# Where the transposition of a unit's exponentials stands: at the head of a slot, or at the end of the slot ahead

## The chip, the cores and the metric

The kernel runs on one core of a Trainium2 chip. The metric is the device time of one execution in microseconds. It computes an attention layer with a sliding window and a few sink keys, and a feed forward layer on its result.

## What is computed

The reference, cut to its core (4 batches, 8 heads, 768 positions, head size 64, `n_sink` 4, `window` 128; 512 columns into 2048 and back):

```python
keep = is_sink | in_window                  # the first 4 keys, and the 128 keys up to the query's own
scores = np.where(keep, scores, -1e9)       # scores = q k^T / 8
a = np.exp(scores - scores.max(-1))
a = a / (a.sum(-1) + 1e-9)
x = (a @ v)                                 # heads side by side: 3072 rows of 512
h = x @ w_in
r = np.maximum(h, 0.0)
out = (s * (r * r) + b) @ w_out
```

## The kernel before

The 3072 rows are worked in 8 chunks of 384 (a batch and a half of its positions). Every float32 operand is split into a high and a low part, and a product is three matmuls (or fewer, with both parts packed into one operand).

**Two streams woven by hand.** `moe_steps` gives 32 steps for a chunk: `l1(f)` makes `h` of 128 of the 2048 columns (12 matmuls, L589), and `l2(f)` adds them into three accumulators `po` (9 matmuls, L608). From the third `l1` on, `l1` and `l2` take turns. Between them stand the slots of the attention of the next chunk; the loop at L768 to L774 issues slot `i` after the first step `j` for which `i * 30 < (j + 1) * (number of slots)`. Chunks 0 and 1 have another, plain attention (`plain_slots`); chunks 2 to 7 have `attn_slots`, which the change touches.

**A slot.** Head `h` has three units (128 queries each), a chunk 24 units, a pair of heads six. Slot `t` works on several units at once:

- `turn` (L324): the transposition, on TensorE, of the exponentials of unit `t - LB` into the last 128 columns of a bank of PSUM, `bank[:, 3 * P:]`.
- `unit_a`: the scores of unit `t` (L303, L304) into the first columns of that same bank, the mask and the maximum on VectorE (L308), the exponential on ScalarE (L314), and two small operations on GpSimd (L317, L318).
- `unit_b`: out of the transposition of unit `t - LB`, the high and low parts `hl` (L337 on VectorE, L339 on ScalarE, L340 on GpSimd; where a unit has no block to its left, L342 and L343 in their place).
- `unit_c`: `o`, the product with the values, of unit `t - LC` (L376, L368). The bank `o` is taken at a head's second unit and read at its third (L384, L385). At a pair's last unit `ts` (L391) is added, and read by L393 and L394.
- `unit_d`: at a pair's last unit, `os` (L402) and `zb` (L404), read by L405 and L406; then `x` of the pair is complete (L407, L408).

With `LB, LC, LD = 3, 6, 2` there are 32 slots. `unit_d` does something in slots 13, 19, 25 and 31.

**The banks.** `ps(...)` takes a tile from `psA`, a pool of five banks of PSUM, for `sc` (the common bank of a slot), `h`, `o`, `ts`, `os` and `zb`. A tile's first write waits until the last reader of the bank's former tile is through. For `sc` the readers are L308 and L337, for `h` L592 and L594. The accumulators `po` have three banks of their own.

**The order.** The framework places semaphores, and a planner of its own orders each engine's instructions: those written earlier go first, but one that the planner's estimate of time sees blocked lets later ones pass. On the chip each engine then works in that order.

Of the kernel before, what the change touches and what calls it, by code (L numbers as in the profile page):

```python
# [15 lines left out]
P = 128  # L16
# [17 lines left out]
RB, VB = 2, 2  # L34
E0 = 8
FN, FB, FC = (4, 2), (6, 6), (9, 10)
LB, LC, LD, L2 = 3, 6, 2, 2


@with_exitstack  # L40
def tile_kernel(ctx, tc, qT, kT, k0, v, vsk, n_sink, window, w, s, b, out):
# [6 lines left out]
    def ps(name):  # L48
        return psA.tile([P, 512], F32, tag="a", name=name)
# [182 lines left out]
    def new_chunk(c):  # L232
        k = Chunk()
        k.c, (k.b, k.half) = c, ORDER[c]
        k.x = [wk.tile([P, NCC, CH], F32R, tag=f"x{i}", name=f"x{i}_{c}") for i in range(2)]
        k.cc, k.xx, k.heads, k.pairs = {}, {}, {}, {}
        return k
# [54 lines left out]
    def unit_a(k, h, i, sc):  # L292

        hd = k.heads[h]
        pp = k.pairs[h // 2]
        g = k.half * BLK + i
        u = (k.c * H + h) * BLK + i
        if k.half == 0:
            c0, n = ((0, 144), (16, 272), (144, 272))[i]
        else:  # L300
            c0, n = ((0, 272), (128, 272), (272, 272))[i]
        qs = slice(i * P, (i + 1) * P)
        nc.tensor.matmul(sc[:, :n], hd.qs[:, qs], hd.kh[:, c0:c0 + n], start=True, stop=False)  # L303
        nc.tensor.matmul(sc[:, :n], hd.qs[:, qs], hd.kl[:, c0:c0 + n], start=False, stop=True)  # L304
        m = m_0 if g == 0 else m_1 if g == 1 else m_odd if g % 2 else m_even
        uu = slice(u, u + 1)
        sm = wk.tile([P, W], F32, name="sm", tag="sm", bufs=SMB)
        nc.vector.tensor_tensor_reduce(out=sm[:, :n], in0=sc[:, :n], in1=m, scale=-0.125, scalar=BIG,  # L308
                                       op0=ALU.add, op1=ALU.min, accum_out=negm[:, uu])

        k.cc[(h, i)] = (sm,) + ((NS, None, 0) if g == 0 else (P, 0, 2 * P) if g % 2 else (P + NS, 0, P))
        s0 = k.cc[(h, i)][3]
        hh = h % 2
        nc.scalar.activation(sm[:, :n], sm[:, :n], AF.Exp, bias=negm[:, uu], scale=-1.0, accum_out=pp.zz[:, i, hh:hh + 1])  # L314
        if g > 0:
            c1, p1 = k.cc[(h, i)][1:3]
            nc.gpsimd.tensor_tensor(out=sm[:, c1:c1 + P], in0=sm[:, p1:p1 + P], in1=sm[:, c1:c1 + P], op=ALU.add)  # L317
        nc.gpsimd.tensor_copy(out=pp.psk[:, i, :6 * NS].rearrange("p (t x) -> p t x", t=3)[:, :, hh * NS:(hh + 1) * NS],  # L318
                              in_=sm[:, s0:s0 + NS].unsqueeze(1).to_broadcast([P, 3, NS]))

    def turn(k, h, i, tp):

        sm, c0 = k.cc[(h, i)][:2]
        nc.tensor.transpose(tp, sm[:, c0:c0 + P], ident)  # L324

    def unit_b(k, h, i, tp):

        sm, c0, p0, _ = k.cc.pop((h, i))
        hd = k.heads[h]
        if i == 0:  # L330
            hd.hl = wk.tile([P, 2, 2 * CH], F32R, name="hl", tag="hl", bufs=HLB)

        a, z = (P if p0 is None else 0), 2 * P
        hi, lo = (hd.hl[:, t, i * z + a:(i + 1) * z] for t in range(2))
        if p0 is not None:
            both = wk.tile([P, 2 * P], F32, tag="two", name="two", bufs=2)
            nc.vector.tensor_tensor(out=both.rearrange("p (s c) -> p s c", s=2), in0=tp.unsqueeze(1).to_broadcast([P, 2, P]), in1=split,  # L337
                                    op=ALU.mult)
            nc.scalar.copy(hi, both)  # L339
            nc.gpsimd.tensor_tensor(out=lo, in0=both, in1=hi.bitcast(F32), op=ALU.subtract)  # L340
        else:
            nc.scalar.copy(hi, tp)  # L342
            nc.vector.tensor_tensor(out=lo, in0=tp, in1=hi.bitcast(F32), op=ALU.subtract)  # L343
        pp = k.pairs[h // 2]
        if h % 2 == 1 and i == BLK - 1:
            zr = wk.tile([P, 2, BLK, 2], F32, tag="zr", name="zr")
            zh = wk.tile([P, BLK, 2], F32R, tag="zh", name="zh")
            nc.vector.tensor_scalar(out=zr[:, 0], in0=pp.zz, scalar1=1e-9, scalar2=None, op0=ALU.add)
            nc.vector.reciprocal(out=zr[:, 1], in_=zr[:, 0])
            nc.vector.tensor_copy(zh, zr[:, 1])  # L350
            nc.gpsimd.tensor_copy(out=pp.psk[:, :, 96:98], in_=zh.bitcast(F32))
            nc.vector.tensor_tensor(out=pp.psk[:, :, 98:100], in0=zr[:, 1], in1=zh.bitcast(F32), op=ALU.subtract)

    def unit_c(k, h, i):

        hd = k.heads[h]
        pp = k.pairs[h // 2]
        cur = i if k.half == 0 else i + 1
        if i == 1:
            hd.o = ps("o")  # L360
            hd.n = 0

        mm = []
        if i == BLK - 1:
            c0 = (2 * i + 1) * P
            nc.tensor.matmul(hd.o[:, i * P:], hd.vv[:, cur, :], hd.hl[:, :, c0:c0 + P], start=False, stop=False)  # L368
        if i > 0:
            mm.append((cur - 1, 2 * i - 1, 2))  # L370
        if i == 1 and k.half == 1:
            mm.append((0, 0, 1))
        for kb, c0, n in mm:
            for t in range(2):
                q0 = c0 // 2 * P
                nc.tensor.matmul(hd.o[:, q0:q0 + n * P], hd.vv[:, kb, :], hd.hl[:, t, c0 * P:(c0 + n) * P],  # L376
                                 start=(hd.n == 0), stop=(i == BLK - 1 and kb == cur - 1 and t == 1))
                hd.n += 1
        if i == BLK - 1:
            a, c = (0, D) if h % 2 == 0 else (D, 0)  # L380
            if h % 2 == 0:
                pp.x = wk.tile([P, CH + P], F32, tag="xm", name="xm", bufs=1)
                pp.y = wk.tile([P, CH + P], F32, tag="y", name="y", bufs=1)
            nc.scalar.copy(pp.y[a:a + D], hd.o[c:c + D])  # L384
            nc.vector.tensor_tensor(out=pp.x[a:a + D], in0=hd.o[a:a + D], in1=pp.y[a:a + D], op=ALU.add)  # L385
            if h % 2 == 1:
                nc.gpsimd.tensor_tensor(out=pp.x[:, CH - P:CH], in0=pp.x[:, CH - P:CH], in1=pp.x[:, CH:], op=ALU.add)
                pp.x = pp.x[:, :CH]
                ts = ps("ts")
                for j in range(BLK):  # L390
                    nc.tensor.transpose(ts[:, j * P:(j + 1) * P], pp.psk[:, j, :], ident)  # L391
                pp.xs = wk.tile([P, CH], F32R, tag="xsk", name="xsk", bufs=1)
                nc.scalar.copy(pp.xs, ts[:, :CH])  # L393
                nc.vector.tensor_tensor(out=pp.xs[32:64], in0=ts[32:64, :CH], in1=pp.xs[32:64].bitcast(F32), op=ALU.subtract)  # L394
# [15 lines left out]
    def attn_slots(c):  # L410
        k = new_chunk(c)
        units, ahead = [], {}
        for pr in range(H // 2):
            h, t0 = 2 * pr, 2 * BLK * pr
            units += [(h + hh, i) for hh in range(2) for i in range(BLK)]
            todo = ((-5, load_pair, pr), (-5, load_keys, h), (-2, load_sinks, pr), (-2, prep_head, h), (-2, load_keys, h + 1),
                    (1, prep_head, h + 1))
            for d, fn, a in todo:
                ahead.setdefault(max(t0 + d, 0), []).append((fn, a))
        n = len(units)  # L420

        def slot(t):
            def f():

                for fn, a in ahead.get(t, ()):
                    fn(k, a)
                bank = ps("sc") if t < n + LB else None
                if 0 <= t - LB < n:
                    turn(k, *units[t - LB], bank[:, 3 * P:])
                if t < n:  # L430
                    unit_a(k, *units[t], bank)
                if 0 <= t - LB < n:
                    unit_b(k, *units[t - LB], bank[:, 3 * P:])
                if 0 <= t - LC < n:
                    unit_c(k, *units[t - LC])
                if 0 <= t - LC - LD < n:
                    unit_d(k, *units[t - LC - LD])
            return f

        return k, [slot(t) for t in range(n + LC + LD)]  # L440


# [300 lines left out]
    k, slots = plain_slots(0)  # L743
# [18 lines left out]
    for c in range(NC_):  # L762
        steps = moe_steps(k.x, store_at(c), wk, before if c == 0 else None, c == NC_ - 1)
        slots = []
        if c + 1 < NC_:
            k, slots = plain_slots(1) if c == 0 else attn_slots(c + 1)
# [58 lines left out]
```

## Time and profile before

| | us |
|---|---|
| median of 3 runs | 745.1 (744.76 to 747.49) |
| the profiled execution, its own time | 745.48 |
| its span, first to last instruction | 743.7 |
| TensorE busy in the span | 707.4 |
| VectorE busy | 507.5 |
| ScalarE busy | 478.7 |
| GpSimd busy | 398.2 |

Times in rows are microseconds from the span's start. PE is TensorE, PEld its weight loads, DVE VectorE, ACT ScalarE, POOL GpSimd. L324 is line 324 of the kernel. An arrow with a name in square brackets says how long the engine stood idle before the row and what released it. The ends of matmuls are modelled and they overlap, so what a matmul costs is read from the distance between starts or ends of neighbours, and a short wait of TensorE may show only there.

### The profile page before, as it was taken

The numbers are of one execution on the slowest core, as the hardware profiler recorded it, in microseconds if no ns is written. First come the engines' busy times: TensorE is split into PE (matmuls) and PEld (weight loads), VectorE is DVE, ScalarE is ACT, GpSimd is POOL, SyncE is SP. The second block draws the span as 40 slices with busy tenths as digits, with TensorE's granted clock in tenths as the row PEclk, the third lists the DMA queues.
The fourth block names the chain that finished last, engine by engine and source line by source line (L and its number), as shares of the span: only waits on it lengthen the run. The fifth ranks groups of instructions, "written<-read, shape, count | busy, mean of one in ns | idle before, by whom it ended". The sixth has DMA issues, their size and how long they took to land.

```text
span 743.7 us, 11974 instructions
## 1 busy us (share of the span) xinstructions
PE 707.4 (95%) x3848; PEld 617.5 (83%) x3848; DVE 507.5 (68%) x1213; ACT 478.7 (64%) x1169; POOL 398.2 (54%) x641
## 2 busy tenths in 40 slices
PE   6788799999999999999999999999999999999996
PEld 3367577789888998899888998899889999889885
DVE  6779999647874778657776678838776568743231
ACT  4978877567774777656774677738675578643222
POOL 2254654358982789626772589816664379710000
PEclk8889989999999999999999999999999999999999
DMA  7845131042221211111111222112111212001001
GB/s 272 339 169 191 33 115 57 27 126 67 62 65 44 70 56 53 44 64 50 54 49 49 73 67 67 46 40 64 55 52 41 86 42 61 9 1 43 1 0 48
DMA packets 27222, 53.03 MB, mean 71 GB/s; under 512 B 3472, under 2 KB 15376, under 8 KB 25232
## 3 DMA queue, kind: packets, MB, share of 16 engines
q1 hardware_dynamic: 27152, 52.18, 21.0%
q8 instruction: 33, 0.54, 0.3%
q14 instruction: 37, 0.30, 0.1%
HBM read 45.88 MB, written 6.29 MB: 70 GB/s over the span
## 4 chain that ended last, share of the span: by engine, by line
PE 67%; DVE 15%; ACT 6%; DMA 4%; issue 3%; POOL 3%; SPq 1%; ACTq 0%; DVEq 0%; POOLq 0%
PE po L608 29%; PE h L589 28%; PE o L376 2%; DVE g L597 2%; DMA vf<-in_v 2%; PE sc L303 2%; PE sc L304 2%; ACT sm L314 2%; DMA w<-in_w 2%; DVE w L214 2%; PE sc L324 2%; DVE wt L213 1%; POOL w L216 1%; DVE r L594 1%; DVE xm L385 1%
## 5 line engine op out<-in xcount | busy, mean ns | idle before, releaser
L589 PE MATMUL h<-x,w 128*128 128x384 f32 x1536 | 296.2, 342 | 3.5 <-DVE hl L343 2.5
L608 PE MATMUL po<-w,g 128*128 128x512 f32 x1152 | 293.2, 400 | 0.0
L589 PEld LDWEIGHTS h<-x,w 128*128 128x128 f32 x1536 | 268.7, 189 | 10.6 <-DVE hl L343 2.9
L608 PEld LDWEIGHTS po<-w,g 128*128 128x128 f32 x1152 | 211.8, 190 | 45.1 <-issue 2.4
L594 DVE SCALAR_TENSOR_TENSOR r<-h,sb,r 128x384 f32<-128x384 f32 x128 | 78.7, 615 | 68.9 <-ACT r L592 67.9
L597 DVE SCALAR_TENSOR_TENSOR g<-r,sb,g 128x384 fp32r<-128x384 f32 x128 | 92.0, 719 | 42.5 <-ACT g L596 41.5
L596 ACT ACTIVATE g<-r,sb 128x384 fp32r<-128x384 f32 x128 | 78.6, 614 | 52.1 <-DVE r L594 51.8
L340 POOL TENSOR_TENSOR hl<-two,hl 128x256 fp32r<-128x256 f32 x128 | 99.4, 777 | 20.8 <-ACT hl L339 18.1
L592 ACT ACTIVATE r<-h 128x384 f32<-128x384 f32 x128 | 62.5, 489 | 66.2 <-PE h L589 65.8
L314 ACT ACTIVATE sm<-sm,negm 128x272 f32<-128x272 f32 (+1 forms) x144 | 73.1, 508 | 45.7 <-DVE negm L308 43.4
L317 POOL TENSOR_TENSOR sm<-sm 128x128 f32<-128x128 f32 x128 | 65.4, 511 | 57.1 <-ACT sm L314 55.2
L308 DVE CUSTOM_DVE_ANT_0 sm<-sc,msk 128x272 f32<-128x272 f32 (+1 forms) x144 | 60.5, 420 | 47.7 <-PE sc L304 46.2
L284 POOL TENSOR_TENSOR kl<-kraw,kh 128x544 fp32r<-128x544 f32 (+1 forms) x48 | 62.5, 1303 | 24.5 <-ACT kh L282 23.9
L289 POOL TENSOR_TENSOR vv<-vraw,vv 128x256 fp32r<-128x256 f32 (+1 forms) x48 | 39.1, 816 | 38.3 <-ACT vv L288 38.0
L216 POOL TENSOR_TENSOR w<-w 128x1024 int32<-128x1024 int32 (+1 forms) x17 | 32.6, 1920 | 45.6 <-DVE w L214 25.1
L318 POOL COPY psk<-sm 128x48 f32<-128x48 f32 x144 | 40.7, 282 | 29.6 <-ACT sm L314 27.3
L337 DVE TENSOR_TENSOR two<-sc,split 128x256 f32<-128x256 f32 x128 | 53.4, 417 | 2.1 <-POOL hl L340 1.1
L339 ACT CAST hl<-two 128x256 fp32r<-128x256 f32 x128 | 50.2, 392 | 6.2 <-DVE two L337 6.2
L303 PE MATMUL sc<-kh,qs 128*128 128x272 f32 (+1 forms) x144 | 50.8, 355 | 0.0
L385 DVE TENSOR_TENSOR xm<-o,y 64x512 f32<-64x512 f32 x48 | 33.1, 689 | 24.1 <-ACT y L384 14.9
L376 PE MATMUL o<-hl,vv 128*128 128x256 f32 (+1 forms) x256 | 44.4, 275 | 0.0
L283 DVE TENSOR_TENSOR qs<-qraw,qs 64x384 fp32r<-64x384 f32 x48 | 38.3, 798 | 5.1 <-ACT qs L279 3.8
(129 smaller groups left out, 915.0 us busy)
## 6 DMA issues: line engine op xcount, KB each, us to landing
w<-in_w SPq DMA_DIRECT2D x15, 1024.0 KB, 9.1
kraw<-in_kT SPq DMA_DIRECT2D x32, 272.0 KB, 2.6
out<-ot SPq DMA_DIRECT2D x24, 256.0 KB, 2.0
qraw<-in_qT SPq DMA_DIRECT2D x24, 192.0 KB, 2.5
vraw<-in_v SPq DMA_DIRECT2D x16, 256.0 KB, 2.6
kraw<-in_kT SPq DMA_DIRECT2D x16, 208.0 KB, 2.4
vsraw<-in_vsk SPq DMA_DIRECT2D x24, 64.0 KB, 1.9
vraw<-in_v SPq DMA_DIRECT2D x8, 192.0 KB, 2.4
```

The costliest lines, as they stand in the source:

```text
L284: nc.gpsimd.tensor_tensor(out=hd.kl[:, :kw], in0=hd.k[:, :kw], in1=hd.kh[:, :kw].bitcast(F32), op=ALU.subtract)
L303: nc.tensor.matmul(sc[:, :n], hd.qs[:, qs], hd.kh[:, c0:c0 + n], start=True, stop=False)
L308: nc.vector.tensor_tensor_reduce(out=sm[:, :n], in0=sc[:, :n], in1=m, scale=-0.125, scalar=BIG, op0=ALU.add, op1=ALU.min, accum_out=negm[: ...
L314: nc.scalar.activation(sm[:, :n], sm[:, :n], AF.Exp, bias=negm[:, uu], scale=-1.0, accum_out=pp.zz[:, i, hh:hh + 1])
L317: nc.gpsimd.tensor_tensor(out=sm[:, c1:c1 + P], in0=sm[:, p1:p1 + P], in1=sm[:, c1:c1 + P], op=ALU.add)
L340: nc.gpsimd.tensor_tensor(out=lo, in0=both, in1=hi.bitcast(F32), op=ALU.subtract)
L589: nc.tensor.matmul(h[:, :CH], weight[f][:, 0, wi, cc * P:(cc + 1) * P], x[xi][:, cc, :], start=(i == 0), stop=(i == 11))
L592: nc.scalar.activation(r, h[:, :CH], AF.Relu, scale=1.0 / WUP)
L594: nc.vector.scalar_tensor_tensor(out=r, in0=h[:, :CH], scalar=sw_ap, in1=r, op0=ALU.mult, op1=ALU.mult)
L596: nc.scalar.activation(gg[:, 0, :], r, AF.Identity, bias=b_ap, scale=1.0)
L597: nc.vector.scalar_tensor_tensor(out=gg[:, 1, :], in0=r, scalar=b_ap, in1=gg[:, 0, :].bitcast(F32), op0=ALU.add, op1=ALU.subtract)
L608: nc.tensor.matmul(po[tb], gg[:, gi, tsl], weight[f][:, 1, wi, :], start=(f == 0 and i == 0), stop=(f == NF - 1 and i == 2))
```

## The change

The bank of a slot is taken at the end of the slot ahead, and the transposition that goes into it is issued there, in front of the feed forward step that stands between the two slots. `unit_c` moves to the front of the slot. The unit that is transposed at the end of slot `t` is `t + 1 - LB`; with `LB` 4 that is `t - 3`, the unit that slot `t` transposed at its head before. `unit_b` and `unit_c` of a unit come one slot later (`LB` 4, `LC` 7), so there are 33 slots in place of 32 over the same steps.

```diff
-LB, LC, LD, L2 = 3, 6, 2, 2
+LB, LC, LD, L2 = 4, 7, 2, 2
...
-                bank = ps("sc") if t < n + LB else None
-                if 0 <= t - LB < n:
-                    turn(k, *units[t - LB], bank[:, 3 * P:])
-                if t < n:
-                    unit_a(k, *units[t], bank)
-                if 0 <= t - LB < n:
-                    unit_b(k, *units[t - LB], bank[:, 3 * P:])
+                if t == 0:
+                    k.bank = ps("sc")
                 if 0 <= t - LC < n:
                     unit_c(k, *units[t - LC])
+                if t < n:
+                    unit_a(k, *units[t], k.bank)
+                if 0 <= t - LB < n:
+                    unit_b(k, *units[t - LB], k.bank[:, 3 * P:])
                 if 0 <= t - LC - LD < n:
                     unit_d(k, *units[t - LC - LD])
+                if t + 1 < n + LB:
+                    k.bank = ps("sc")
+                if 0 <= t + 1 - LB < n:
+                    turn(k, *units[t + 1 - LB], k.bank[:, 3 * P:])
```

## Rows read from the trace of the kernel before

**Rows 1.** The page: each engine's busy time, and the shares of the chain that ended last, by engine.

```profile
PE 707.4 (95%) x3848; PEld 617.5 (83%) x3848; DVE 507.5 (68%) x1213; ACT 478.7 (64%) x1169; POOL 398.2 (54%) x641
...
PE 67%; DVE 15%; ACT 6%; DMA 4%; issue 3%; POOL 3%; SPq 1%; ACTq 0%; DVEq 0%; POOLq 0%
```

**Rows 2.** What TensorE waited for between 150 and 700 us: total us, times, longest. These two are the whole list.

```profile
PE h L589 <- DVE hl L343: 2.5, 2, 1.2
PE zb L404 <- DVE r L594: 1.3, 5, 0.3
```

**Rows 3.** Groups of instructions on TensorE between 150 and 700 us: count, busy us, mean ns, idle before. The transposition of the change, and `zb`.

```profile
L324 PE MATMUL sc<-identr,sm 128*128 128x128 f32 x144 | 39.2, 272 | 0.0
L404 PE MATMUL zb<-xsk,sel 128*128 128x384 f32 x24 | 9.4, 392 | 1.7 <-DVE r L594 1.3
```

**Rows 4.** The chain of waits through an ordinary slot and the steps around it: start, us, what.

```profile
249.45 2.12 PE h L589 x12
251.58 0.11 PE sc L324
251.69 0.13 PE sc L303
251.81 0.13 PE sc L304
251.94 2.11 PE po L608 x9
```

**Rows 5.** Slot 13 of chunk 3, with `unit_d`, between an `l1` and an `l2` step: instructions in order of time.

```profile
272.60 0.69 PE L589 MATMUL h<-x,w 128*128 128x384 f32 x3
...
273.50 0.56 PE L376 MATMUL o<-hl,vv 128*128 128x256 f32 x4
...
273.90 0.39 PE L402 MATMUL os<-xsk,vs 128*128 128x384 f32 x1
...
274.13 0.34 PE L404 MATMUL zb<-xsk,sel 128*128 128x384 f32 x1
...
274.25 0.43 DVE L308 CUSTOM_DVE_ANT_0 sm<-sc,msk 128x272 f32<-128x272 f32 x1
274.31 2.27 PE L608 MATMUL po<-w,g 128*128 128x512 f32 x9
...
274.76 0.62 DVE L594 SCALAR_TENSOR_TENSOR r<-h,sb,r 128x384 f32<-128x384 f32 x1
...
275.29 0.41 DVE L337 TENSOR_TENSOR two<-sc,split 128x256 f32<-128x256 f32 x1
...
275.62 0.55 DVE L405 TENSOR_TENSOR xm<-os,xm 128x384 f32<-128x384 f32 x1
```

**Rows 6.** The same slot in chunk 4, where the first half of a batch is worked.

```profile
360.00 0.61 DVE L594 SCALAR_TENSOR_TENSOR r<-h,sb,r 128x384 f32<-128x384 f32 x1
360.07 0.87 PE L608 MATMUL po<-w,g 128*128 128x512 f32 x3
```

**Rows 7.** Slot 17 of chunk 3, with `ts`, ahead of an `l1` step.

```profile
283.22 0.49 PE L391 MATMUL ts<-identr,psk 128*128 128x128 f32 x3
...
283.29 0.42 DVE L337 TENSOR_TENSOR two<-sc,split 128x256 f32<-128x256 f32 x1
...
283.47 0.60 PE L589 MATMUL h<-x,w 128*128 128x384 f32 x2
```

**Rows 8.** Slot 19 of chunk 3, with `unit_d`, ahead of an `l1` step.

```profile
288.87 0.61 DVE L594 SCALAR_TENSOR_TENSOR r<-h,sb,r 128x384 f32<-128x384 f32 x1
288.89 0.39 PE L402 MATMUL os<-xsk,vs 128*128 128x384 f32 x1
...
289.54 0.44 PE L404 MATMUL zb<-xsk,sel 128*128 128x384 f32 x1 [0.26 <-DVE r L594]
...
289.97 0.59 PE L589 MATMUL h<-x,w 128*128 128x384 f32 x2
```

**Rows 9.** The end of slot 19 of chunk 4 and what TensorE does behind it.

```profile
374.02 0.40 PE L376 MATMUL o<-hl,vv 128*128 128x256 f32 x2
...
374.54 0.44 PE L404 MATMUL zb<-xsk,sel 128*128 128x384 f32 x1
374.82 0.28 PE L368 MATMUL o<-hl,vv 128*128 128x256 f32 x1
374.94 0.40 PE L376 MATMUL o<-hl,vv 128*128 128x256 f32 x2
376.56 0.62 PE L589 MATMUL h<-x,w 128*128 128x384 f32 x2 [1.23 <-DVE hl L343]
```

**Rows 10.** The end of a `vv` and of a low part `hl` on GpSimd in chunk 4, and the product that reads that `hl`.

```profile
365.25 0.60 POOL L289 TENSOR_TENSOR vv<-vraw,vv 128x192 fp32r<-128x192 f32 x1
...
366.72 0.74 POOL L340 TENSOR_TENSOR hl<-two,hl 128x256 fp32r<-128x256 f32 x1
...
368.41 0.28 PE L368 MATMUL o<-hl,vv 128*128 128x256 f32 x1
```

**Rows 11.** Busy time of each engine while chunk 3's units are worked: the stretch, its length, PE, PEld, DVE, ACT and POOL, each with its count, the granted clock, the DMA share and GB/s.

```profile
247.00:296.00 49.00, 48.74 (x280) 43.90 (x280) 38.76 (x101) 36.97 (x100) 42.56 (x74) 1.00 0.20 59
```

**Rows 12.** What the queue that issues the loads waited for: total us, times, longest.

```profile
SPq L261 <- POOL kl L284: 164.7, 43, 12.2
SPq L248 <- POOL vv L289: 115.1, 20, 12.4
```

## The prediction

> **What bounds the kernel now.** I read the page first. TensorE is busy for 707.4 of the 743.7 us, VectorE, the next, for 507.5, and two thirds of the chain that ended last are matmuls [rows 1]. So an edit is worth what it adds to or takes from TensorE's order, in work or in waiting. Next I read what TensorE waits for while the attention units run: between 150 and 700 us two entries, 3.8 us together, and both are waits for a bank of the pool `psA`, for `h` behind L343 and for `zb` behind L594 [rows 2]. No entry names the exponentials, the low parts or a load. The reader is to see that a transposition never waited there for its input: L324 has 144 instructions and no idle time before them [rows 3]. Then the chain through an ordinary slot, which gives the prices: transposition 0.11 us, the two score matmuls 0.13 each, a feed forward step 2.11 [rows 4]. Last the slots at a pair's end, where the banks run out [rows 5 to 9].
>
> **The transposition itself.** It is the same instruction 144 times, of the same unit behind the same slot. It costs 0.11 us between its neighbours [rows 4], 144 x 0.11 = 15.8 us, before and after. A short wait for input that vanished would be a gain, but there is none [rows 3], so this term is 0. The move issues no DMA. `unit_c` ahead of the scores is also the same work in another place: 0. The 33rd slot adds no matmul, since the units are still 24 a chunk.
>
> **One slot later for `unit_b` and `unit_c`.** The values `vv` are held one slot longer, about 2.5 us (a step and an ordinary slot, [rows 4]). A tight one, in chunk 4, is ready at 365.85 [rows 10] and first read by the product L376 at 374.02 [rows 9], so 8 us of cover stand against 2.5. On the loads' queue the wait for `vv` (115.1 us in 20 waits) and that for `kl` (164.7 in 43) are long already [rows 12] and none of it reaches TensorE [rows 2]: 0, and if that cover were gone, up to 2.5 us at a head. The low parts keep three slots from `unit_b` to `unit_c`, less the slot's own scores, 0.25 us. The tightest in rows ends at 367.46 and is read at 368.41, a cover of 0.95 us [rows 10]: 0, with GpSimd at 42.56 of 49 us in the heavy stretch [rows 11] as the risk.
>
> **The bank that is held longer.** This is the part that I price. A slot's bank was taken at the slot's head, and its transposition and scores were written together. Now the bank is written a step earlier and stands idle through the step: 2.11 us, and `unit_c` besides, for every slot with scores, because L308 still has to wait for them. The pool has five banks. At an ordinary slot a free one is at hand. At a pair's end it is not. In slot 13 of chunk 3, when `zb` is issued, five are occupied: the slot's own `sc` (L337 ends at 275.70), `o`, `os` (L405 ends at 276.17), `zb`, and the `h` of the step before, whose L594 ends at 275.38 [rows 5]. Before, that cost nothing, because an `l2` step came next and takes no bank. After the change the transposition comes next and takes a sixth. It waits from 274.31, where `po` starts now, to 275.38: 1.07 us, and the nine `po` matmuls stand behind it in TensorE's queue. In chunk 4 the same wait is 360.61 - 360.07 = 0.54 us [rows 6]. Chunks 2, 3, 5 and 7 work a second half like chunk 3, chunks 4 and 6 a first half: 4 x 1.07 + 2 x 0.54 = 5.4 us for this slot, which becomes slot 14.
>
> The next pair's end becomes slot 20. By the loop's rule slot `i` stands behind step `30 i / 33`, rounded down: slot 14 behind step 12 and slot 20 behind step 18, both `l1` steps with an `l2` next, so slot 20 now stands as slot 13 did. I price it the same, 5.4 us. Slot 26 has no scores: L337 can read the transposition at once, during the step, so the bank is back in time, and I take 0. Its upper bound is 1.07 in six chunks, 6.4 us. The slot with `ts` that shares its gap with another becomes slot 12. At the like place before, slot 17, five banks are taken when `h` starts at 283.47, and the next comes free with L337 at 283.71 [rows 7]: 0.24 x 6 = 1.4 us. All these waits have 0 as their lower bound: the planner may let other matmuls pass.
>
> **What the new spacing takes away.** Slot 19 stood ahead of an `l1` step, behind an `l2`. There `zb` starts 0.65 us after `os` [rows 8], against 0.23 in slot 13 [rows 5], and the following step 0.43 after `zb` against 0.18: 0.42 + 0.25 = 0.67 us lost. I assume it in the four second-half chunks, 2.7 us. In chunk 4 `h` waits 1.23 us for a bank [rows 9], in two chunks 2.5 [rows 2]. As slot 20, ahead of an `l2` step, neither has its cause any more: -5.2 us, with 0 as the other bound.
>
> **The sum.** 5.4 + 5.4 + 1.4 - 5.2 = +7.0 us on the profiled execution's 745.5 us. That execution stands 0.4 us above the median of the runs, so I predict 752 us.
>
> **A rule beside a row.** `zb` waited five times for a bank, 1.3 us in all, at pair ends of different chunks [rows 2]. The Trainium skill, Perfetto Trace Analysis, section Optimization Strategy, says that the same gap returning on the engine that ought to be saturated can mean that there is too little SBUF or PSUM for the next tile. The rows agree, since L594, which ends the wait, is the reader of a former bank. By that rule a longer hold makes the bubble larger; by the row's size alone, 1.3 us, the change would be worth nothing either way, about 745 us.
>
> **Rivals.**
>
> *The banks come in time and only the new spacing counts: faster.* The planner lets the `po` matmuls pass a transposition that it sees blocked, and the 5.2 us of the old slot 19 are still saved: 745.5 - 5.2 = 740.3 us. For it: behind slot 19 of chunk 4 the planner did let later work pass, the products L368 and L376 of slot 20 stand ahead of the blocked `h` [rows 9]. Against it: `h` then waited 1.23 us more on the chip with `po` matmuls to be had, so the planner's estimate was short by about that much, and a wait of 1.07 may look like none to it. It decides from the point where the planner sees the transposition blocked for the whole wait.
>
> *Both nearly cancel: no change.* The planner sees part of the waits, and half of the 12.2 us stays: 745.5 + 6.1 - 5.2 = 746.4 us. For it speaks the same row; against it, that `zb` follows straight on its `os` in slot 19 though it waits [rows 8].
>
> *The change does dearer harm.* Slot 26 waits too and the old slot 19's losses come back in slot 20 because the `h` of the step just before holds its bank even later: 745.5 + 12.2 + 6.4 = 764 us. GpSimd adds to this if the units, which now come every 30/33 of a step rather than every 30/32, find it full: it is at 87% there [rows 11], and the low parts' cover is 0.95 us [rows 10]. Against it: slots 24 to 27 have no scores, so their banks are short lived.
>
> **How the numbers follow.** I give the forecast 50%, the faster rival 20%, the cancelling 18%, the dearer 12%. About 0.5%, 3.7 us, is what a measurement of this kernel can tell from no change. The forecast falls beyond it on the slow side in nine of ten cases, the faster rival on the fast side in about four of five, the dearer always. That makes 57% slower, 16% faster, 27% within. The range goes from the faster rival, 740 us, to the dearer, 764 us, which leaves out the tails of both.
>
> **What would show it.** Right: TensorE's waits list L324 behind L594, L308 or L337, at slots 14 and 20, about 1 us each, and `h` behind L343 is gone from it; L324 keeps its count and its 0.11 us. If L324 has no idle time and `po` matmuls stand ahead of it at pair ends, the planner has moved it and the faster rival holds. If products L368 and L376 wait for L340, the low parts were the weak place and my sum lacks a term. The prediction is wrong in its core if the time between 150 and 700 us grows without waits for banks.

## The result

The changed kernel takes 749.64 us in the median against 744.93 before, a ratio of 1.0063 (95% interval 1.0041 to 1.0085): 0.6% slower. The prediction said 752 us, from the profiled execution's +7.0 us; measured in medians it is +4.7.

Executions of one and the same kernel spread by about 1% here (741.7 to 748.8 for the one before), and part of that lies in the first 150 us, which the change does not touch (the first `h` of chunk 1 starts at 152.5 us in the profile before and at 150.3 in the one after). So beside the ratio I use the distance from the first `h` matmul of a chunk to the first of the next, read from the trace of one execution of each kernel. Six such intervals hold attention units (chunks 2 to 7); the fourth column tells which unit chunk.

| feed forward of chunk | before, us | changed, us | units of chunk | difference |
|---|---|---|---|---|
| 1 | 86.9 | 88.2 | 2, second half | +1.3 |
| 2 | 86.2 | 87.9 | 3, second half | +1.7 |
| 3 | 85.7 | 84.7 | 4, first half | -1.1 |
| 4 | 86.3 | 87.8 | 5, second half | +1.6 |
| 5 | 85.8 | 84.7 | 6, first half | -1.1 |
| 6 | 86.0 | 87.6 | 7, second half | +1.6 |
| sum | 516.9 | 520.8 | | +3.9 |

Two starts of the changed kernel, chunk 2 and chunk 3, whose distance is 326.34 - 238.46 = 87.88 us:

```profile
238.46 0.86 PE L592 MATMUL h<-x,w 128*128 128x384 f32 x4
...
326.34 0.86 PE L592 MATMUL h<-x,w 128*128 128x384 f32 x4
```

**The profile after.** In the changed kernel the `h` matmuls are L592, the `po` matmuls L611, the reading of `h` L595 and L597; lines up to L426 are as before. What TensorE waits for between 150 and 700 us, the whole list, beside [rows 2]:

```profile
PE sc L324 <- DVE r L597: 7.2, 8, 1.0
PE sc L324 <- DVE xm L385: 1.1, 2, 0.6
PE zb L404 <- DVE hl L343: 0.5, 2, 0.2
```

Both entries of before are gone, `h` behind L343 and `zb` behind the square (L597 here, L594 before: the last reader of an `h`). In their place the transposition waits, 8 times for 7.2 us, behind that square. It does not read `h`; it waits for that tile's bank. The third line is new too, 0.2 us at `zb` in each first-half chunk. The group of the transposition in the same stretch, beside [rows 3]:

```profile
L324 PE MATMUL sc<-identr,sm 128*128 128x128 f32 x144 | 40.0, 278 | 8.3 <-DVE r L597 7.2 <-DVE xm L385 1.1
```

Still 144 instructions, now with 8.3 us of idle time ahead of them. Slot 14 of chunk 3, in order of time, to be laid beside [rows 5]:

```profile
273.52 0.33 PE L404 MATMUL zb<-xsk,sel 128*128 128x384 f32 x1
...
274.15 0.61 DVE L597 SCALAR_TENSOR_TENSOR r<-h,sb,r 128x384 f32<-128x384 f32 x1
...
274.68 0.43 DVE L308 CUSTOM_DVE_ANT_0 sm<-sc,msk 128x272 f32<-128x272 f32 x1
...
274.81 0.33 PE L324 MATMUL sc<-identr,sm 128*128 128x128 f32 x1 [0.96 <-DVE r L597]
...
274.90 0.95 PE L611 MATMUL po<-w,g 128*128 128x512 f32 x3
```

`zb` takes the fifth bank, L597 ends at 274.76, and 0.05 us later the transposition starts; the `po` matmuls that stood straight behind `zb` before now stand behind it. Slot 20 of the same chunk does the same:

```profile
291.92 0.34 PE L404 MATMUL zb<-xsk,sel 128*128 128x384 f32 x1
...
292.40 0.62 DVE L597 SCALAR_TENSOR_TENSOR r<-h,sb,r 128x384 f32<-128x384 f32 x1 [1.11 <-ACT r L595]
...
293.07 0.33 PE L324 MATMUL sc<-identr,sm 128*128 128x128 f32 x1 [0.82 <-DVE r L597]
```

In a first-half chunk TensorE's order is another one. Behind slot 14 of chunk 4:

```profile
360.91 0.44 PE L404 MATMUL zb<-xsk,sel 128*128 128x384 f32 x1 [0.22 <-DVE hl L343]
361.19 0.64 PE L611 MATMUL po<-w,g 128*128 128x512 f32 x2
361.66 0.30 PE L324 MATMUL sc<-identr,sm 128*128 128x128 f32 x1
```

Here the planner put two `po` matmuls ahead of the transposition, and it does not wait; behind slot 20 of this chunk the order is the same. The chunk pays once, in the pair of slots 22 and 23 that share a gap between steps, where a bank `o` is late:

```profile
384.52 0.30 PE L324 MATMUL sc<-identr,sm 128*128 128x128 f32 x1 [0.55 <-DVE xm L385]
```

### The profile page after: what moved, and what is told of

Its sections match the earlier page's. It is cut to its first block, busy times and chain, and to the rows that moved or that the text cites. A ratio compares the mean times of both kernels' runs of the same rounds, so it can differ in the third digit from the quotient of the medians.

```text
span 745.3 us, 11938 instructions
## 1 busy us (share of the span) xinstructions
PE 704.0 (94%) x3848; PEld 620.0 (83%) x3848; DVE 512.8 (69%) x1213; ACT 481.4 (65%) x1169; POOL 396.5 (53%) x641
## 4 chain that ended last, share of the span: by engine, by line
PE 68%; DVE 16%; ACT 5%; POOL 3%; DMA 3%; issue 2%; SPq 1%; ACTq 0%; POOLq 0%; DVEq 0%
PE po L611 30%; PE h L592 28%; DVE g L600 2%; PE o L376 2%; PE sc L324 2%; DMA vf<-in_v 2%; PE sc L303 2%; PE sc L304 2%; DVE r L597 2%; DMA w<-in_w 2%; DVE qs L283 1%; POOL w L216 1%; DVE xm L385 1%; DVE wt L213 1%; DVE two L337 1%
## 5 line engine op out<-in xcount | busy, mean ns | idle before, releaser
L592 PE MATMUL h<-x,w 128*128 128x384 f32 x1536 | 299.8, 344 | 0.2
L611 PE MATMUL po<-w,g 128*128 128x512 f32 x1152 | 297.2, 403 | 0.0
L592 PEld LDWEIGHTS h<-x,w 128*128 128x128 f32 x1536 | 268.7, 189 | 7.0 <-issue 1.0
L611 PEld LDWEIGHTS po<-w,g 128*128 128x128 f32 x1152 | 211.5, 190 | 44.4 <-issue 2.6
L597 DVE SCALAR_TENSOR_TENSOR r<-h,sb,r 128x384 f32<-128x384 f32 x128 | 78.6, 614 | 82.8 <-ACT r L595 82.4
L600 DVE SCALAR_TENSOR_TENSOR g<-r,sb,g 128x384 fp32r<-128x384 f32 x128 | 101.3, 792 | 42.3 <-ACT g L599 41.5
L340 POOL TENSOR_TENSOR hl<-two,hl 128x256 fp32r<-128x256 f32 x128 | 99.7, 779 | 26.1 <-ACT hl L339 25.3
L595 ACT ACTIVATE r<-h 128x384 f32<-128x384 f32 x128 | 62.5, 488 | 78.0 <-PE h L592 76.3
L317 POOL TENSOR_TENSOR sm<-sm 128x128 f32<-128x128 f32 x128 | 67.9, 530 | 57.9 <-ACT sm L314 55.2
L308 DVE CUSTOM_DVE_ANT_0 sm<-sc,msk 128x272 f32<-128x272 f32 (+1 forms) x144 | 60.4, 420 | 38.6 <-PE sc L304 30.5
L284 POOL TENSOR_TENSOR kl<-kraw,kh 128x544 fp32r<-128x544 f32 (+1 forms) x48 | 61.0, 1271 | 23.6 <-ACT kh L282 23.4
L337 DVE TENSOR_TENSOR two<-sc,split 128x256 f32<-128x256 f32 x128 | 53.3, 418 | 2.6 <-POOL hl L340 2.2
L289 POOL TENSOR_TENSOR vv<-vraw,vv 128x256 fp32r<-128x256 f32 (+1 forms) x48 | 35.1, 733 | 36.2 <-ACT vv L288 36.2
L324 PE MATMUL sc<-identr,sm 128*128 128x128 f32 x144 | 40.0, 278 | 8.3 <-DVE r L597 7.2
L385 DVE TENSOR_TENSOR xm<-o,y 64x512 f32<-64x512 f32 x48 | 33.1, 689 | 18.7 <-POOL x L408 10.7
L303 PE MATMUL sc<-kh,qs 128*128 128x272 f32 (+1 forms) x144 | 42.6, 298 | 0.0
```

The lines of the kernel that those rows point to most:

```text
L284: nc.gpsimd.tensor_tensor(out=hd.kl[:, :kw], in0=hd.k[:, :kw], in1=hd.kh[:, :kw].bitcast(F32), op=ALU.subtract)
L592: nc.tensor.matmul(h[:, :CH], weight[f][:, 0, wi, cc * P:(cc + 1) * P], x[xi][:, cc, :], start=(i == 0), stop=(i == 11))
L595: nc.scalar.activation(r, h[:, :CH], AF.Relu, scale=1.0 / WUP)
L597: nc.vector.scalar_tensor_tensor(out=r, in0=h[:, :CH], scalar=sw_ap, in1=r, op0=ALU.mult, op1=ALU.mult)
L600: nc.vector.scalar_tensor_tensor(out=gg[:, 1, :], in0=r, scalar=b_ap, in1=gg[:, 0, :].bitcast(F32), op0=ALU.add, op1=ALU.subtract)
L611: nc.tensor.matmul(po[tb], gg[:, gi, tsl], weight[f][:, 1, wi, :], start=(f == 0 and i == 0), stop=(f == NF - 1 and i == 2))
```

## The experiments

Theory A: the price is that a bank of the pool is held through a step, so that at a pair's end there is none for the transposition. Rivals: B, the spacing (33 slots) and the later `unit_b` and `unit_c` cost by themselves; C, `unit_c` first in the slot costs; D, the price is spread evenly over the transpositions; E, the transposition ahead costs by its place in TensorE's order. "Six intervals" is the sum of the table above for that kernel.

| kernel | ratio to before (95% interval) | six intervals, us |
|---|---|---|
| before | 1 | 516.9 |
| the change | 1.0063 (1.0041 to 1.0085) | 520.8 |
| e1, at its own head behind pair ends | 0.9988 (0.9962 to 1.0015) | 515.8 |
| e2, before with `LB`, `LC` one later | 1.0301 (1.0264 to 1.0338) | 538.4 |
| e3, the change with 32 slots | 1.0269 (1.0234 to 1.0305) | 536.4 |
| e4, before with `unit_c` first | 1.0054 (1.0030 to 1.0077) | 522.4 |
| e5, the change, all at their own heads | 0.9984 (0.9958 to 1.0009) | 514.0 |
| e6, the change, `h` freed early | 1.0198 (1.0158 to 1.0238) | 524.4 |
| e7, before, `h` freed early | 1.0324 (1.0287 to 1.0361) | 534.5 |
| e8, e1 with `h` freed early | 1.0184 (1.0146 to 1.0223) | 522.4 |
| e9, e5, ahead at pair ends alone | 1.0126 (1.0095 to 1.0157) | 525.1 |
| e10, the change without `zb` | 1.0021 (1.0000 to 1.0042) | 518.3 |
| e11, e5 without `zb` | 0.9990 (0.9966 to 1.0014) | 514.3 |
| e12, the change, behind six `po` | 0.9996 (0.9977 to 1.0015) | 517.2 |

**The change without its name.** In e5 `take(t)`, which takes the slot's bank and issues its transposition, stands at the head of the slot; all else of the change stays (the definition of `take` is left out here).

```diff
-                if t == 0:
-                    k.bank = ps("sc")
+                take(t)
                 if 0 <= t - LC < n:
                     unit_c(k, *units[t - LC])
...
-                if t + 1 < n + LB:
-                    k.bank = ps("sc")
-                if 0 <= t + 1 - LB < n:
-                    turn(k, *units[t + 1 - LB], k.bank[:, 3 * P:])
```

> The changed kernel with the one thing of its name undone: every bank is taken, and every transposition issued, at the head of its own slot, in front of unit_c. LB 4, LC 7, 33 slots and unit_c ahead of the scores stay. Theory A (a bank held through the step): the waits of L324 behind L594 at slots 14 and 20 are gone, 1.0 and 0.8 us in each of four second-half chunks, and a second-half chunk takes about 86 us in place of 87.8: ratio 0.993 to 1.000. Theory B (spacing, lateness and unit_c first do the harm by themselves, as the kernel with unit_c first alone, 1.0054, may suggest): ratio 1.004 to 1.008.

The ratio is 0.9984, inside theory A's bounds, and the interval excludes B's. TensorE's list of waits, whole:

```profile
PE o L376 <- DVE xm L385: 1.5, 3, 0.7
```

No transposition waits. So the transposition ahead of the step alone is worth 520.8 - 514.0 = +6.9 us in the six intervals, and the rest of the change 514.0 - 516.9 = -3.0 us. The ratios say the same of the first, 1.0063 against 0.9984; of the second they can't tell, since e5's interval holds 1.

**Where in the chunk it costs.** e1 takes it back behind some slots only, e9 adds it to e5 behind the pair ends only. The condition in e1 also holds for slots 2 and 8, where no pair ends, so five slots were put back in it and not three.

```diff
 # e1, the changed kernel
-                if t == 0:
-                    k.bank = ps("sc")
+                if t == 0 or (t - 1 - LC - LD) % (2 * BLK) == 2 * BLK - 1:
+                    take(t)
...
+                if (t - LC - LD) % (2 * BLK) != 2 * BLK - 1:
+                    take(t + 1)
 # e9, the kernel e5
-                take(t)
+                if t - 1 not in (14, 20, 26):
+                    take(t)
...
+                if t in (14, 20, 26):
+                    take(t + 1)
```

> The changed kernel, but behind the three slots 14, 20 and 26 in which a pair's os and zb are issued, the next slot's bank is taken and its transposition issued at the head of that next slot, as before the change. All else (33 slots, unit_c first, the transposition ahead of the step at every other slot) stays. Theory A (the bank): the loss is L324 waiting for a bank behind those slots, about 1.0 and 0.8 us at slots 14 and 20 of the four second-half chunks, so these waits are gone, a second-half chunk takes 85.5 to 86 us from one first h to the next where the changed kernel takes about 87.8, and the kernel comes out below the one before: ratio 0.992 to 0.997. Theory B (spacing and lateness: 33 slots in the same steps, unit_b and unit_c one slot later): nothing of that is undone, ratio stays at about 1.006.

> The kernel e5 (all of the change but the transposition ahead of the step), with the bank taken and the transposition issued ahead behind slots 14, 20 and 26 alone, three of a chunk's 27. Theory A: nearly the whole price sits at these three, because five banks are taken there; L324 waits 0.8 to 1.0 us at two of them in each second-half chunk, and the six chunks with units take 4 to 6 us longer than in e5: ratio to the kernel before 1.003 to 1.007. Theory D (the price is spread over all slots, 0.05 us at each of 144): about 3 of 27 of it, ratio 0.998 to 1.000.

e1 gets 5.0 of the 6.9 us back. Theory B's 1.006 is excluded; but it came out level with the kernel before, not below it, as theory A had asked. Its waits, whole:

```profile
PE sc L324 <- DVE xm L385: 2.3, 5, 0.7
PE h L596 <- DVE xm L385: 2.1, 4, 0.7
PE zb L404 <- DVE hl L343: 0.5, 2, 0.2
```

The waits behind the square are gone, and a part of them comes back elsewhere: `h` now waits four times for the bank that L385 reads. e9 costs more than the whole change, 525.1 us, with the transposition ahead at 3 slots of 27. That ends theory D; but it is 11.1 us above e5, where theory A had put 4 to 6. Its waits:

```profile
PE sc L324 <- DVE r L601: 6.6, 8, 1.0
PE h L596 <- DVE two L337: 5.8, 5, 1.3
```

The first line is that of the changed kernel. The second, 5.8 of the 11.1 us, is new: behind slot 26, ahead of an `l1` step, `h` waits for L337. In e9 slot 26 still transposes at its own head, so L337 reads that bank late; in the changed kernel it was transposed a step earlier and L337 is through. So the price is set by what else holds banks at that moment.

**One bank fewer.** e10 is the changed kernel and e11 the kernel e5, both without `zb`: the normalisation is not applied.

```diff
-            zb = ps("zb")
-            nc.tensor.matmul(zb[:, :CH], sel, pp.xs, start=True, stop=True)
...
-            nc.vector.tensor_tensor(out=pp.x, in0=zb[:, :CH], in1=pp.x, op=ALU.mult)
```

> The changed kernel without zb: the matmul L404 and the multiplication L406 are left out, so that the normalisation by the sum of the exponentials is not applied. One bank fewer is needed at a pair's end; TensorE has 24 x 0.18 = 4.2 us less to do. Theory A: four banks are taken where five were when the transposition comes, so no wait of L324 behind the square at slots 14 and 20, and the distance to the next kernel, the same without the transposition ahead, is under 2 us in the six chunks, where it was 6.9 with zb. Theory E (the transposition ahead costs by its place in TensorE's order, not by a bank): the distance stays at about 7 us.

> The kernel e5 (all of the change but the transposition ahead of the step) without zb: L404 and L406 are left out, as in the run before, so that the normalisation is not applied. It is the partner of that run: theory A expects the two within 2 us of each other in the six chunks with units, theory E 7 us apart. Against e5 it should be faster by the 4.2 us of matmuls and by what zb waits there, 1 to 2 us: ratio to the kernel before 0.990 to 0.993.

The waits of e10, whole:

```profile
PE o L376 <- DVE xm L385: 3.4, 3, 1.2
PE h L589 <- DVE xm L385: 3.1, 4, 0.8
PE h L589 <- DVE r L594: 2.3, 5, 0.5
PE sc L324 <- DVE xm L385: 0.4, 2, 0.2
PE sc L324 <- DVE hl L343: 0.4, 2, 0.2
```

With one bank fewer needed, the transposition does not wait behind the square any more, as A said; its place in the order is the same. But the two kernels stand 518.3 - 514.3 = 3.9 us apart, neither under 2 nor 7. Other tiles wait for banks now, and that accounts for a part only: e10's list adds up to 9.6 us and e11's to 7.8, so some 2 us of the distance stand in neither. By this pair alone theory E is not excluded as a part of the price. And e11 is not faster than e5 although TensorE has 4.2 us less to do; its list has

```profile
PE o L376 <- DVE xm L385: 5.6, 3, 2.0
```

That part of the expectation failed.

**The same wait, covered.** In e12 the transposition behind slots 14 and 20 is issued inside the following `l2` step, behind six of its nine `po` matmuls, much as the planner did by itself in the first-half chunks.

```diff
+                if t in (14, 20):
+                    mid.append(lambda: take(t + 1))
+                else:
+                    take(t + 1)
 # in l2, behind the matmuls of token block tb
+                if tb == 1:
+                    while mid:
+                        mid.pop()()
```

> The changed kernel, but behind slots 14 and 20 the bank is taken and the transposition issued inside the l2 step that follows, behind six of its nine po matmuls (1.4 us), which need no bank of the pool. Theory A: the bank that the transposition waited for, 0.96 and 0.82 us, is back by then, so the waits of L324 behind the square are gone and the po matmuls no longer stand behind them; the four second-half chunks lose their 2.2 us of waits and the six chunks together take 511 to 514 us, where the kernel before took 516.9 and the changed one 520.8: ratio 0.991 to 0.997, the fastest of these kernels. If the wait is not for a bank that comes back with time, it stays where the transposition is now, and the ratio stays above 1.000.

Slot 14 of chunk 3 in e12, `po` being L621:

```profile
275.94 0.33 PE L404 MATMUL zb<-xsk,sel 128*128 128x384 f32 x1
276.11 1.57 PE L621 MATMUL po<-w,g 128*128 128x512 f32 x6
277.51 0.27 PE L324 MATMUL sc<-identr,sm 128*128 128x128 f32 x1
277.54 0.95 PE L621 MATMUL po<-w,g 128*128 128x512 f32 x3
```

No wait stands there; L607, the square in e12, ends at 277.19. The six intervals fall from 520.8 to 517.2 us, and the ratio from 1.0063 to 0.9996. The wait was for something that comes back with time, as a bank does. The rest of what I expected, 511 to 514 us, did not come; the list of waits has

```profile
PE sc L324 <- DVE xm L385: 2.2, 5, 0.7
PE h L602 <- DVE xm L385: 2.2, 4, 0.7
```

**The bank named by the wait.** In e6, e7 and e8 the square reads `r` twice in place of `h` and `r`, so `h` is free after ScalarE (e6 the changed kernel, e7 the one before, e8 as e1).

```diff
-nc.vector.scalar_tensor_tensor(out=r, in0=h[:, :CH], scalar=sw_ap, in1=r, ...)
+nc.vector.scalar_tensor_tensor(out=r, in0=r, scalar=sb[:, 0:1], in1=r, ...)
```

> The changed kernel with one operand of the square changed: it multiplies s * r * r from r in SBUF where it multiplied s/256 * h * r with h in PSUM (the same value). So h's bank is free after ScalarE's L595, and no longer after VectorE's turn for the square, which stands 0.5 to 1 us later. Theory A: the waits of L324, 7.2 us in 8 behind that square, shrink to less than half, since then an h bank or the slot's own bank comes back first; ratio to the kernel before 0.998 to 1.003. If the waits are not for h's bank, they stay, and the ratio stays at 1.006.

> The kernel before with the same operand changed. Theory A: its waits for a bank at zb behind the square (1.3 us idle, about 2.7 with what the pitch shows) go, those of h behind L343 may stay: ratio 0.993 to 0.999. If reading both inputs from SBUF makes the square slower on VectorE (615 ns before), that shows in its mean.

> Both: the changed kernel, the transposition ahead of the step at every slot but those behind a pair's end, and h's bank freed by ScalarE. Theory A: waits for banks down to 2 us or less between 150 and 700 us, ratio 0.990 to 0.997, the best of these kernels.

All three are 2 to 3% slower, against every expectation. In the mean the square itself became dearer. Its group in e6:

```profile
L597 DVE SCALAR_TENSOR_TENSOR r<-r,sb 128x384 f32<-128x384 f32 x128 | 107.6, 840 | 77.7 <-ACT r L595 77.0
```

840 ns against 614 in the changed kernel: 29 us more on VectorE. Of the 9.9 us between the spans of e6 and of the changed kernel 6.5 lie in the feed forward of chunk 0, outside the six intervals. What e6 still tells is which bank it was. The 7.2 us of L324 behind the square are gone, and behind L595, `h`'s only reader left, stands

```profile
PE sc L324 <- ACT r L595: 0.7, 3, 0.3
```

As comparisons of times the three settle nothing.

**The other parts of the change.** e4 is the kernel before with `unit_c` first; e2 the kernel before with `LB, LC = 4, 7`; e3 the changed kernel with `LB, LC = 3, 6`.

```diff
 # e4
+                if 0 <= t - LC < n:
+                    unit_c(k, *units[t - LC])
                 bank = ps("sc") if t < n + LB else None
 # e2, the kernel before
-LB, LC, LD, L2 = 3, 6, 2, 2
+LB, LC, LD, L2 = 4, 7, 2, 2
 # e3, the changed kernel
-LB, LC, LD, L2 = 4, 7, 2, 2
+LB, LC, LD, L2 = 3, 6, 2, 2
```

> The kernel before with LB 4 and LC 7 alone: the transposition stays at the head of its slot and its bank is taken there, but transposition, unit_b and unit_c of a unit come one slot later and there are 33 slots. Theory A: no bank is held through a step, so no L324 wait; the old slot 19's losses (h behind L343 in the first-half chunks, zb behind L594) go or shrink with the new spacing: ratio 0.992 to 1.000. Theory B: all the harm is here, ratio 1.004 to 1.010.

> The changed kernel with LB 3 and LC 6: 32 slots as before, unit_b and unit_c at their old places, and the transposition still issued ahead of the step, so now one slot earlier than before. Theory A: the bank is held through a step as in the changed kernel; behind slot 13 L324 waits about 1 us, and slots 19 and 25 stand ahead of an l1 step, where both L324 and h need a bank, 1 to 1.5 us each; and the exponentials, ready 1.3 to 2 us before their transposition at the tightest slots before, now come late at some slots, which gives L324 waits for L317: ratio 1.008 to 1.020. Theory B: with the old spacing back the harm is gone, ratio 0.998 to 1.002.

> The kernel before with unit_c moved to the head of the slot, ahead of the transposition, and nothing else. Theory A: same matmuls, no longer hold of the slot's bank; only the bank o is taken 0.36 us earlier in the slot: ratio 0.998 to 1.002. Theory C (the order within the slot is what costs, because the scores and so L308 come 0.4 us later in a slot): ratio 1.004 or more, with L308 and the exponentials later by that much.

e2 did not test what it was for. With `unit_c` last in the slot and one slot later, the sink columns `psk` of a pair are overwritten by those of the pair after next before `ts` reads them, so that part of the computation is another one, and `ts` waits for the overwriting:

```profile
PE ts L391 <- POOL psk L318: 23.1, 12, 3.3
```

It shows why `unit_c` has to go first once it comes a slot later. e5 took its place as the test of theory B.

e3 is 2.7% slower with the old spacing, more than I had put. B's 1.000 is excluded. The expected waits for the exponentials hardly came (0.2 us behind L317); the larger part is banks, `h` behind L337 at slots that stand ahead of an `l1` step:

```profile
PE h L592 <- DVE two L337: 12.2, 11, 2.0
PE sc L324 <- POOL hl L340: 5.3, 4, 1.3
```

L340 reads no bank, so what the four waits of the second line were for stays open.

e4 is 0.54% slower, which theory A had not foreseen. It speaks for C in the old spacing; but its waits too are for banks. The largest entry of its list, and the wait at slot 20 of chunk 3:

```profile
PE sc L324 <- DVE two L337: 4.7, 4, 1.2
...
293.31 0.30 PE L324 MATMUL sc<-identr,sm 128*128 128x128 f32 x1 [1.19 <-DVE two L337]
```

and on VectorE ahead of that L337:

```profile
289.36 1.50 DVE L283 TENSOR_TENSOR qs<-qraw,qs 64x384 fp32r<-64x384 f32 x1
...
291.33 1.15 DVE L597 SCALAR_TENSOR_TENSOR g<-r,sb,g 128x384 fp32r<-128x384 f32 x1
292.39 0.43 DVE L308 CUSTOM_DVE_ANT_0 sm<-sc,msk 128x272 f32<-128x272 f32 x1
...
292.75 0.41 DVE L337 TENSOR_TENSOR two<-sc,split 128x256 f32<-128x256 f32 x1
```

The planner gave VectorE another order there, with L283 between a square and the next L308; in the kernel before L283 starts at 284.95, ahead of that square. That this order is what makes the difference was not tried by itself. And 2.3 of the 5.5 us in the six intervals lie in chunk 4's units, where the granted clock fell (last section). With 33 slots, in e5, `unit_c` nearly first goes with a kernel no slower than before; what it costs within that was not tried.

## Why the prediction was right, and where its terms were off

**The mechanism.** Slot, instruction and releaser are the ones forecast: L324 behind the square of `h`, at slots 14 and 20. The distance between e5 and the changed kernel, 6.9 us, is that one move; e9 and e12 place it at the pair ends, e10 shows that a bank is what is missing.

**Second-half chunks.** Slot 14 was put at 1.07 us; the trace has 0.96 of idle time. Slot 20 was put at the same and has 0.82. With the 0.67 us that the old slot 19 lost and no longer loses, that gives about +1.1 us of idle time; the intervals show +1.3 to +1.7. The 0.24 us for the slot with `ts` stand in no row, and slot 26 cost nothing, as taken.

**First-half chunks.** Here the size of the term failed. I priced 2 x 0.54 of waits for each chunk; there are none, since two `po` matmuls stand ahead of the transposition at both slots. That is the faster rival's mechanism, and in two chunks of six it was the right one. `h` behind L343 is gone as forecast, 1.23 us each. In its place stand 0.55 us behind L385 and 0.2 at `zb`, which I had not listed. The intervals fall by 1.1 us where my sum had about +0.1.

**The sum.** Waits +12.2 and spacing -5.2 gave +7.0. The runs show +6.9 for the transposition ahead and -3.0 for all the rest, +3.9 us. So the first term was too large by 5.3 us, 2.2 of it the first-half waits, 1.4 the slot with `ts` and 1.4 the second-half waits, 0.96 and 0.82 for twice 1.07 (0.3 stay unplaced); the spacing's gain was too large by 2.2 us, and e5 shows where. In the first-half chunks it is 2.0 us each below the kernel before, more than the 1.23 that I took. In chunk 7 it is 0.6 us below, about the 0.67 forecast. But in chunks 2, 3 and 5 it is 0.3, 0.6 and 0.7 us above, and there `o` waits 0.66, 0.34 and 0.55 us behind L385, a wait that my sum lacks. The one of chunk 3:

```profile
306.62 0.68 PE L376 MATMUL o<-hl,vv 128*128 128x256 f32 x4 [0.34 <-DVE xm L385]
```

Whether `unit_c` first, which I had put at 0, makes that wait was not tried. A harm 5.3 us too large and a gain 2.2 us too large offset each other in part, so it is in part luck that the sum came as near as it did.

**What I did not see.** A bank wait removed is not a bank wait saved. In e1, e10 and e12 the transposition's waits behind the square go to zero, and 4 to 7 us of waits behind L385, the reader of `o`, stand in the lists, where the changed kernel has 1.1. My reading is that VectorE is behind at those places, and TensorE waits for it at whichever tile next finds no bank; no run made VectorE faster there. The Trainium skill, Perfetto Trace Analysis, section Optimization Strategy, says that a gap that repeats on the engine that should be saturated can mean too little SBUF or PSUM for the next tile. The eight waits of L324 at two pair ends of four chunks agree, 0.82 to 0.96 us each in chunk 3. The row by itself, 1.3 us of `zb`, had pointed to no change; the rule was nearer.

None of these kernels is faster than the one before by more than its interval: e5 comes nearest, 0.9984 (0.9958 to 1.0009).

## What to carry to other kernels

When TensorE is the bound and its tiles come from one small pool of banks, an instruction moved ahead is priced by how long it waits for the next bank to come free, at the places where the pool is already empty (here 0.8 to 1.0 us at two slots of a second-half chunk): count there who holds each bank and when its last reader ends. Look for work that needs no bank and can stand in front of it, as six `po` matmuls did in e12. And expect a part of a wait that is removed to return at the next place where the reading engine is behind.

## What the runs showed of the hardware

Two things that I had not expected. In e4, after TensorE had stood idle for 0.52 us ahead of `zb` and 1.08 us ahead of the next `h`, the granted clock fell for about 3 us; the middle row of three stretches in chunk 4 has it at 0.51, the lower level of 1.2 GHz:

```profile
370.00:378.00 8.00, 6.41 (x37) 5.42 (x35) 6.95 (x20) 5.91 (x17) 5.72 (x12) 1.00 0.31 81
378.00:381.20 3.20, 3.20 (x11) 3.20 (x12) 1.56 (x5) 1.42 (x4) 2.49 (x5) 0.51 0.22 75
381.20:390.00 8.80, 8.80 (x51) 7.96 (x50) 5.70 (x15) 6.28 (x17) 4.34 (x9) 0.98 0.11 32
```

The twelve `h` matmuls of that stretch, and twelve of chunk 3 in the same kernel:

```profile
289.39 2.38 PE L589 MATMUL h<-x,w 128*128 128x384 f32 x12
...
377.90 3.92 PE L589 MATMUL h<-x,w 128*128 128x384 f32 x12 [1.08 <-DVE hl L343]
```

That is 1.5 us beside the waits themselves. In chunk 6 of the same profile the same two waits stand and the clock stays up, so the waits alone do not settle it.

The other is the square of `h` with both inputs in SBUF: its mean rose from 614 ns to 840, but its median did not. Shortest, median and longest in ns, first in e6, then in the changed kernel:

```profile
L597 DVE SCALAR_TENSOR_TENSOR r<-r,sb x128: 604/619/2782, 48.4 to 743.1; 128x384 f32<-128x384 f32 x128
...
L597 DVE SCALAR_TENSOR_TENSOR r<-h,sb,r x128: 604/617/621, 48.7 to 733.4; 128x384 f32<-128x384 f32 x128
```

In e6's trace 55 of the 128 squares take more than 650 ns, and each of these overlaps an instruction on GpSimd; the 47 with GpSimd idle for all but 5% of their time take 616 ns in the mean and 619 at most, the 42 with GpSimd busy for over 95% of it 937. In the changed kernel, with `h` in PSUM, 49 squares have GpSimd busy for over 95% of their time and take 613 ns in the mean. So in these traces the square with both inputs in SBUF is dearer only where GpSimd works beside it; no run took GpSimd's work away to try it.
